# Attention, GLU and soft-MoE on one core: the value products of both blocks of a pair of heads in one group

## The chip, the core and the metric

The kernel runs on one NeuronCore of a Trainium2 chip. A core has five engines that run their own streams of instructions and meet at semaphores: TensorE (PE: matmuls and transposes), VectorE (DVE), ScalarE (ACT), GpSimd (POOL) and SyncE (SP), which here does nothing but issue DMAs. Matmuls write to PSUM, from where ACT and DVE copy results to SBUF. The metric is the device time of one execution in microseconds (us); a profiled execution, in which a hardware profiler records each instruction, gives the trace.

## What is computed

```python
attn = softmax(causal(q @ k.T / sqrt(D)) + decay_bias(s)) @ v    # B, H, S, D = 4, 8, 576, 64
x = attn, heads side by side                                      # 2304 tokens x 512
x = ((x @ w1) * (x @ w2)) @ w3 @ w_out                            # 512 -> 1024 -> 1024 -> 512
logits = x @ phi                                                  # 8 experts with 4 slots each
slots = softmax(logits over tokens).T @ x
y = relu(slot @ ew1[e]) @ ew2[e]                                  # for each expert's slots
out = softmax(logits over slots) @ y
```

The bias of a pair of positions is the difference of a running sum of max(s, 0), cut at zero. The weights of the middle part come as 64-bit floats.

## The kernel before, in words

**Items.** Attention goes through 40 items (ITEMS, L265). The 576 tokens of a head are five tiles: tile 0 has 64 tokens, tiles 1 to 4 have 128 each (QT, L32). Items 0 to 15 are the eight heads of batch 0 in two halves: tiles 0, 1, 2 of each head, then tiles 3 and 4. Items 16 to 39 are heads 8 to 31 with all five tiles. Heads 2m and 2m+1 make a pair, so there are twelve pairs of whole heads, items 16/17 to 38/39. The tokens lie in two blocks (BLK, L34): block 0 is tiles 0 to 2, 320 tokens; block 1 is tiles 3 and 4, 256 tokens.

**Steps of an item.** `att_scores` (L341) multiplies q and k: PE writes the sum of a product with `qa` and one with `qb` to `sc_ps`; DVE (L344) adds the mask and takes the row maximum nmax; ACT (L349) takes the exponential. `att_norm` divides on POOL (L362). `att_transpose` turns the result on PE (L377, `pt_ps`), copied by ACT to `pt` (L379), and the diagonal parts (L391, `ptd_ps`), copied to `ptd` (L393). `att_pv` (L395 on) multiplies by the values v.

**The value products.** For a pair n, n+1 and one block, `att_pv` takes an accumulator `x_ps` from the two PSUM buffers with the tag `acc` (PB, L78: four of tag `sg` for `sc_ps` and `gl`, two of `acc`, two of `tp`). Each product of the first head (e = 0) writes partitions 0 to 63, its twin of the second head (e = 1) partitions 64 to 127. Block 0 has ten products, block 1 twelve; each is two MATMUL records in the trace, as the operands are f32. `group` (L104) gives a list of products a high priority and chains them so that their order holds. The first of a list waits in addition for the copies of pt and ptd of both heads. Behind the products ACT copies the accumulator to `x[:, 0]` (L426, a CAST), and DVE writes the rest to `x[:, 1]` (L427). z_ps and ct_ps of the soft-MoE use the same two buffers of tag `acc`.

**What runs beside it.** While the items of one batch go on, the GLU of an earlier batch runs (`glu_half`, L430: twelve products `gl` to one buffer of `sg`, L439; ACT copies the first half to `a`, L445; DVE multiplies, L457, to gT, gU or gC), the soft-MoE's sums (`slot_...` functions: `gn_ps`, `lg`, `z_ps`, `ct_ps`), and the conversion of the weights: SP fetches words (L178, `raw_w`, `raw_wo`, `raw_w3t`), ACT (L186, L197) and DVE (L198, L201) convert them, SP stores some (L229).

**What sets the order.** `att_steps` writes a list of steps with a cost each; `weave` (L677) merges two lists in the ratio of their costs, and a scheduler turns this program into an order for PE, ACT, DVE and POOL, using priorities and its own picture of when operands are ready. SP alone keeps the order of the program. Its order in each item is: the values of a pair (L290, two buffers `v`, so that it waits for the value products of the pair two before), the decay rows for `qb` (L306), q and k (`raw`, L282), words (L178). When the last items are done, the loads of the tail begin with L828, whose place waits for the last value product.

Of the kernel before, what the change touches and what calls it, by code (L numbers as in the profile page):

```python
# [10 lines left out]
F32 = mybir.dt.float32  # L11
# [5 lines left out]
ALU = mybir.AluOpType  # L17
# [30 lines left out]
def attn_glu_softmoe_kernel(  # L48
# [31 lines left out]
    def psum(tag, name):  # L80
        return ps.tile([P, 512], F32, tag=tag, name=name, bufs=PB[tag])
# [310 lines left out]
                t["diag", j] = k  # L392
            t["turned", "d"] = nc.scalar.copy(out=ptd[:, : len(own)].rearrange("p j q -> p (j q)"), in_=dg[:, 64 : 64 * len(own) + 64])  # L393

    def att_pv(n, blk):  # L395

        b, c = divmod(ITEMS[n][0] // 2, H // 2)
        t0, nt, tiles = BLK[blk]
        acc = psum("acc", f"x_ps_{n}_{blk}")
        products = []  # L400

        def add(cols, weights, vs, start, stop):
            for e in range(2):
                t = hd[n + e]
                products.append((acc[64 * e : 64 * e + 64, cols], vs(t["v"], e), weights(t), start, stop))

        def diag(i, start, stop):
            d0 = sum(QT[i]) - 64 - t0
            add(slice(d0, d0 + 64), lambda t: t["ptd"][:, t["diag", i]], lambda v, e: v[:, 2 * i, e], start, stop)

        if tiles[0] == 0:
            diag(0, True, True)
        for j in range(tiles[-1]):

            own = [i for i in tiles if i > j]
            p0 = PT[own[0]][0] + PT[own[0]][1] * j
            add(
                slice(QT[own[0]][0] - t0, sum(QT[own[-1]]) - t0),
                lambda t: t["pt"][:, p0 : p0 + len(own)].rearrange("p i q -> p (i q)"),
                lambda v, e: v[:, 2 * j + 1, e], j == 0, False,  # L420
            )
        for i in tiles[-2:]:
            diag(i, False, i == tiles[-1])
        group(products, [hd[n + e]["turned", i] for e in range(2) for i in (tiles[-1], "d")])
        x = x_t[b, blk, c]
        nc.scalar.copy(out=x[:, 0], in_=acc[:, :nt])  # L426
        nc.vector.tensor_tensor(out=x[:, 1], in0=acc[:, :nt], in1=x[:, 0].bitcast(F32), op=ALU.subtract)  # L427


    gts = {}  # L430
# [207 lines left out]
    def att_steps(ap):  # L638

        groups = [[] for _ in range(B + 1)]  # L640
        N = len(ITEMS)
        for n in range(N + 1):
            tiles = ITEMS[n][1] if n < N else ()
            old = [i for i in ITEMS[n - 1][1] if i] if 0 < n <= N else []
            sc = [(0.2 + 0.3 * i, lambda i=i, n=n: att_scores(n, i, ap)) for i in tiles]
            tr = [(0.2 + 0.3 * i, lambda i=i, n=n: att_transpose(n - 1, i, ap)) for i in old]
            norm = [(0, lambda n=n: att_norm(n - 1))] if 0 < n <= N else []
            prep = [(0, lambda n=n: att_values(n + 1, ap))] if n + 1 < N else []
            d = FAR if n + FAR < NF32 else 1 if NF32 <= n + 1 < N else 0
            if d:  # L650
                prep += [(0, lambda m=n + d: att_prep(m, ap))]
            d = FAR + 1 if n + FAR + 1 < NF32 else 2 if NF32 <= n + 2 < N else 0
            if d:
                prep += [(0, lambda m=n + d: att_fetch(m, ap))]
            blks = [k for k in range(2) if BLK[k][2][0] in ITEMS[n - 1][1]]
            pv = [(1.4, lambda n=n, k=k: att_pv(n - 2, k)) for k in blks] if n > 0 and n % 2 == 0 else []
            groups[min(B, max(0, (n - 1) // H))] += [
                *sc[:1], *norm, *sc[1:2], *prep, *sc[2:3], *tr[:1], *sc[3:4], *tr[1:2], *sc[4:], *tr[2:], *pv
            ]
        return groups  # L660
# [457 lines left out]
```

## Time and profile before

| | |
|---|---|
| median of 3 runs | 562.74 us (562.33 to 567.34) |
| profiled execution, its own time | 565.44 us |
| its span in the trace | 563.6 us |
| mean granted clock of TensorE | 0.981 of full speed |
| instructions | 11844, of them 4288 MATMUL records |
| PE busy | 520.0 us, 92% of the span |
| weight loads (PEld), which overlap PE | 433.9 us |
| DVE, ACT, POOL busy | 316.2, 310.0, 196.7 us |
| bytes moved | 118.03 MB, 209 GB/s over the span |

The page gives one line per view; in the timeline a row is a run of like instructions, with its start, its length, engine, line, operation, tiles and count, and in brackets the idle time of the engine just before it and what ended it. PE's matmuls are pipelined, so the length of a row reaches into the next; the distance of two starts is what a piece of work costs. In the list of waits stands the idle time of an engine in front of a line, summed, with how often and the longest.

### The profile page before, as it was taken

To read this page: it belongs to the slowest core of one execution; us is meant where nothing else is said; L and a number is where in the kernel's file an instruction comes from. 1 tells how busy PE (TensorE), PEld (TensorE's weight loads), DVE (VectorE), ACT (ScalarE), POOL (GpSimd) and SP (SyncE) were. 2 spreads that over 40 slices of the span, in tenths; PEclk is the share of its full clock that TensorE was granted. 3 is DMA by queue.
4 is the path that set the end of the run, shared out by engine and by line. 5 is a ranking of instruction groups with operands and counts; after the bars stand their busy time and mean duration, and the time that the engine had idled before them with its cause. 6 is when DMAs were issued, how large, how long until landed. Compare 5 with 4: busy or idle time off the path is not lost. (4 is left out here: it accounts for less than half of the span.)

```text
span 563.6 us, 11844 instructions
## 1 busy us (share of the span) xinstructions
PE 520.0 (92%) x4288; PEld 433.9 (77%) x4288; DVE 316.2 (56%) x966; ACT 310.0 (55%) x845; POOL 196.7 (35%) x247
## 2 busy tenths in 40 slices
PE   3789899998979999899899999999999999999993
PEld 2566688787768897889889889889988999853452
DVE  7568696889964385736574657446631311243333
ACT  4576586788865675646566567357833321321222
POOL 5475464438745374253354444333210000000000
PEclk9997899999979999999999999999999999999998
DMA  5765966868654173345646563555330999689977
GB/s 157 237 179 178 261 203 215 287 219 261 191 201 119 39 220 109 130 135 179 206 136 213 168 197 104 166 167 172 113 113 1 391 413 381 233 300 421 421 296 244
DMA packets 38809, 118.03 MB, mean 209 GB/s; under 512 B 4224, under 2 KB 10560, under 8 KB 35296
## 3 DMA queue, kind: packets, MB, share of 16 engines
q1 hardware_dynamic: 36832, 113.74, 58.8%
q10 hardware_dynamic: 1920, 3.54, 2.5%
q8 instruction: 34, 0.56, 0.4%
q14 instruction: 23, 0.19, 0.1%
HBM read 102.11 MB, written 11.60 MB: 202 GB/s over the span
## 5 line engine op out<-in xcount | busy, mean ns | idle before, releaser
L439 PE MATMUL gl<-x,w12t 128*128 128x320 f32 (+1 forms) x1536 | 238.3, 304 | 1.3 <-DVE nmax L344 0.7
L439 PEld LDWEIGHTS gl<-x,w12t 128*128 128x128 f32 x1536 | 212.2, 191 | 10.0 <-issue 4.3
L362 POOL TENSOR_SCALAR sc<-sc,rinv 128x64 f32<-128x64 f32 (+4 forms) x160 | 92.4, 594 | 53.9 <-DVE rinv L359 39.2
L349 ACT ACTIVATE sc<-sc,nmax 128x64 f32<-128x64 f32 (+4 forms) x160 | 89.5, 560 | 32.2 <-DVE nmax L344 31.6
L317 POOL TENSOR_TENSOR qa<-raw,qa 64x576 fp32r<-64x576 f32 x24 | 36.5, 1522 | 144.1 <-DVE qa L311 138.3
L344 DVE CUSTOM_DVE_ANT_0 sc<-sc_ps,mask 128x64 f32<-128x64 f32 (+4 forms) x160 | 64.8, 424 | 32.1 <-PE sc_ps L341 29.0
L379 ACT COPY pt<-pt_ps 128x128 f32<-128x128 f32 (+3 forms) x128 | 52.2, 423 | 27.1 <-PE pt_ps L377 16.3
L377 PE MATMUL pt_ps<-ident,sc 128*128 128x128 f32 x320 | 56.8, 288 | 4.9 <-ACT pt L379 2.3
L341 PE MATMUL sc_ps<-qa 128*128 128x64 f32 (+1 forms) x144 | 46.6, 336 | 6.0 <-DVE nmax L344 2.5
L377 PEld LDWEIGHTS pt_ps<-ident,sc 128*128 128x128 f32 x320 | 38.8, 145 | 17.3 <-issue 10.0
L341 PE MATMUL sc_ps<-qb 68*128 68x64 f32 (+1 forms) x144 | 44.2, 310 | 4.2 <-issue 4.2
L110 PE MATMUL x_ps<-pt,v 128*64 128x256 f32 (+1 forms) x384 | 47.5, 353 | 0.0
L445 ACT COPY a<-gl 128x256 f32<-128x256 f32 (+1 forms) x64 | 25.3, 398 | 38.5 <-PE gl L439 34.8
L341 PE MATMUL sc_ps<-raw 68*128 68x288 f32 (+4 forms) x96 | 35.5, 514 | 11.1 <-DMA raw<-rows 9.6
L990 POOL MEMSET ht<- 128x1024 f32 x2 | 1.9, 954 | 107.3 <-DVE ew L894 98.4
L186 ACT ACTIVATE w_w<-raw_w 128x512 f32<-128x512 f32 x32 | 21.6, 676 | 31.6 <-DMA raw_w<-in_w 31.6
L314 POOL TENSOR_TENSOR qb<-raw,qa 64x576 fp32r<-64x576 f32 x24 | 38.2, 1590 | 2.2 <-PE gl L439 0.5
L110 PEld LDWEIGHTS x_ps<-pt,v 128*64 128x64 f32 x384 | 32.0, 138 | 6.7 <-issue 1.0
L341 PEld LDWEIGHTS sc_ps<-qa 128*128 128x128 f32 x144 | 27.7, 192 | 9.1 <-DVE nmax L344 3.5
L427 DVE TENSOR_TENSOR x<-x_ps,x 128x320 fp32r<-128x320 f32 (+1 forms) x32 | 14.0, 455 | 36.2 <-ACT x L426 36.1
L341 PEld LDWEIGHTS sc_ps<-raw 68*128 68x128 f32 x96 | 21.2, 259 | 16.3 <-issue 12.1
L341 PEld LDWEIGHTS sc_ps<-qb 68*128 68x128 f32 x144 | 28.0, 194 | 4.6 <-issue 4.4
(180 smaller groups left out, 785.4 us busy)
## 6 DMA issues: line engine op xcount, KB each, us to landing
ew<-in_ew SPq DMA_DIRECT2D x27, 1024.0 KB
raw_w<-in_w SPq DMA_DIRECT2D x32, 512.0 KB
raw<-in_qk SPq DMA_DIRECT2D x24, 576.0 KB
v<-in_v SPq DMA_DIRECT2D x16, 576.0 KB
raw_w3t<-in_w3t SPq DMA_DIRECT2D x16, 512.0 KB
raw_wot<-in_wot SPq DMA_DIRECT2D x8, 512.0 KB
raw_wo<-in_wo SPq DMA_DIRECT2D x8, 512.0 KB
w_d<-w_w SPq DMA_DIRECT2D x8, 512.0 KB
```

The costliest lines, as they stand in the source:

```text
L110: mm = nc.tensor.matmul(out_, lhs, rhs, start=start, stop=stop)
L186: nc.scalar.activation(out=w, in_=hi.bitcast(F32), func=AF.Copy, scale=F64_SCALE)
L314: nc.gpsimd.tensor_tensor(out=qb[0:64, 1, :q1], in0=rk[0:64, :q1], in1=qa[0:64, 1, :q1].bitcast(F32), op=ALU.subtract)
L317: nc.gpsimd.tensor_tensor(out=qa[64:, 0, q0:q1], in0=rq[64:, q0:q1], in1=qa[64:, 0, q0:q1].bitcast(F32), op=ALU.subtract)
L341: nc.tensor.matmul(pp[:r, : z - a], x[:, 0, q0 : q0 + r], x[:, 1, a:z], start=x is mul[0], stop=x is mul[-1])
L344: nc.vector.tensor_tensor_reduce(out=sc[:r, a:z], in0=pp[:r, : z - a], in1=hd["mask"][:r, m0 : m0 + z - a], scale=-0.125, scalar=3.0e38 if ...
L349: nc.scalar.activation(out=sc[:r, :W], in_=sc[:r, :W], func=AF.Exp, bias=nmax[:r, i : i + 1], scale=-1.0, accum_out=rsum[:r, i, 0:1],)
L362: nc.gpsimd.tensor_scalar(out=sc, in0=sc, scalar1=rinv[:, i : i + 1], scalar2=1.0, op0=ALU.mult, op1=ALU.mult)
L377: nc.tensor.transpose(tp[:, j * P : (j + 1) * P], sc[:, j * P : (j + 1) * P], ident)
L379: t["turned", i] = nc.scalar.copy(out=pt[:, p0 : p0 + step * (i - 1) + 1 : step], in_=tp[:, : i * P].rearrange("p (j q) -> p j q", q=P))
L439: nc.tensor.matmul(acc[:, :nt], w12_t[fc][:, wi, n, kc], x_t[b, blk, kc][:, xi], start=k == 0, stop=k == 3 * KC - 1)
L445: nc.scalar.copy(out=a_sb[:, :nt], in_=acc[:, :nt])
```

## The change

`att_pv` takes a list of blocks in place of one. For the pairs of items 0 to 15, which have one block each, the program is as it was. For the twelve pairs of items 16 to 39 one call makes both blocks: it takes both `acc` buffers, puts the 22 products in one list, block 0 first, and hands them to one `group`; behind it stand the copy and the subtraction of block 0, then those of block 1. The first product waits for the turned copies of the last tile of both heads and of ptd. In `att_steps` one step of cost 2.8 stands where two of 1.4 stood. The lines behind `att_pv` move down by five: L439 of before is L444 of after, L426 is L431.

```diff
-    def att_pv(n, blk):
+    def att_pv(n, blks):
         b, c = divmod(ITEMS[n][0] // 2, H // 2)
-        t0, nt, tiles = BLK[blk]
-        acc = psum("acc", f"x_ps_{n}_{blk}")
-        products = []
+        products, accs = [], {}
+        for blk in blks:
+            t0, nt, tiles = BLK[blk]
+            acc = accs[blk] = psum("acc", f"x_ps_{n}_{blk}")
...
-        group(products, [hd[n + e]["turned", i] for e in range(2) for i in (tiles[-1], "d")])
-        x = x_t[b, blk, c]
-        nc.scalar.copy(out=x[:, 0], in_=acc[:, :nt])
-        nc.vector.tensor_tensor(out=x[:, 1], in0=acc[:, :nt], in1=x[:, 0].bitcast(F32), op=ALU.subtract)
+        last = BLK[blks[-1]][2][-1]
+        group(products, [hd[n + e]["turned", i] for e in range(2) for i in (last, "d")])
+        for blk in blks:
+            nt, acc, x = BLK[blk][1], accs[blk], x_t[b, blk, c]
+            nc.scalar.copy(out=x[:, 0], in_=acc[:, :nt])
+            nc.vector.tensor_tensor(out=x[:, 1], in0=acc[:, :nt], in1=x[:, 0].bitcast(F32), op=ALU.subtract)
...
-            pv = [(1.4, lambda n=n, k=k: att_pv(n - 2, k)) for k in blks] if n > 0 and n % 2 == 0 else []
+            pv = [(1.4 * len(blks), lambda n=n, k=blks: att_pv(n - 2, k))] if n > 0 and n % 2 == 0 else []
```

The order of POOL is the same in both kernels, and that of SP too but for names of buffers. ACT has 703 rows and DVE 944 in both, in another order. PE has 1803 rows before and 1814 after.

The first place is items 30/31 on PE (x_ps_0 is block 0, x_ps_1 block 1; numbers behind the names tell buffers apart; ptd_3874 and pt_3873 are of head 0 of the pair, ptd_4030 and pt_4029 of head 1; lg_1 is a sum of the soft-MoE). Before:

```order
L110 MATMUL x_ps_0_4128<-ptd_3874,v_3627 64x64
L110 MATMUL x_ps_1_4156<-pt_3873,v_3627 64x256
L110 MATMUL lg_1_4286<-gT_1_0_3515,v_sb 32x256
L110 MATMUL lg_1_4286<-gT_1_1_3563,v_sb 32x256
L110 MATMUL lg_1_4286<-gT_1_2_3682,v_sb 32x256
L110 MATMUL lg_1_4286<-gT_1_3_3784,v_sb 32x256
L110 MATMUL lg_1_4286<-gU_1_4_3940,v_sb 32x256 x2
L110 MATMUL lg_1_4286<-gU_1_6_4113,v_sb 32x256 x2
L110 MATMUL x_ps_1_4156<-pt_4029,v_3627 64x256
```

After:

```order
L110 MATMUL lg_1_4286<-gT_1_0_3515,v_sb 32x256
L110 MATMUL lg_1_4286<-gT_1_1_3563,v_sb 32x256
L110 MATMUL lg_1_4286<-gT_1_2_3682,v_sb 32x256
L110 MATMUL lg_1_4286<-gT_1_3_3799,v_sb 32x256
L110 MATMUL lg_1_4286<-gU_1_4_3940,v_sb 32x256 x2
L110 MATMUL lg_1_4286<-gU_1_6_4113,v_sb 32x256 x2
L110 MATMUL x_ps_0_4128<-ptd_3874,v_3627 64x64
L377 MATMUL pt_ps_1_4237<-ident,sc_3983 128x128
L110 MATMUL x_ps_0_4128<-ptd_4030,v_3627 64x64
L110 MATMUL x_ps_0_4128<-pt_3873,v_3627 64x256
L110 MATMUL x_ps_0_4128<-pt_4029,v_3627 64x256
```

The eight lg products, which stood between the first two products and the others, now stand ahead of the pair. The first product of head 0 stands alone, with one transpose behind it, and then the other 21 stand in a row.

The second place is items 24/25 on PE (gl_0_4_1 and gl_0_5_0 are two halves of a GLU of block 0, with 12 products each; sc_ps_0_0 and sc_ps_1_0 are the scores of tiles 0 and 1 of the item after next). Before:

```order
L439 MATMUL gl_0_4_1_3202<-x_0_1_1312,w12t_662 128x320 x3
L110 MATMUL x_ps_0_3041<-ptd_2774,v_2576 64x64
L110 MATMUL x_ps_1_3059<-pt_2773,v_2576 64x256
L110 MATMUL x_ps_0_3041<-ptd_2939,v_2576 64x64
L110 MATMUL x_ps_0_3041<-pt_2773,v_2576 64x256
L110 MATMUL x_ps_0_3041<-pt_2938,v_2576 64x256
L110 MATMUL x_ps_0_3041<-pt_2773,v_2576 64x128
L110 MATMUL x_ps_0_3041<-pt_2938,v_2576 64x128
L110 MATMUL x_ps_1_3059<-pt_2938,v_2576 64x256
```

After:

```order
L444 MATMUL gl_0_4_1_3202<-x_0_3_1960,w12t_662 128x320 x3
L341 MATMUL sc_ps_0_0_3232<-qa_3124 128x64
L341 MATMUL sc_ps_0_0_3232<-qb_3123 128x64
L444 MATMUL gl_0_5_0_3237<-x_0_0_1090,w12t_759 128x320 x3
L444 MATMUL gl_0_5_0_3237<-x_0_1_1312,w12t_759 128x320 x3
L444 MATMUL gl_0_5_0_3237<-x_0_2_1623,w12t_759 128x320 x3
L444 MATMUL gl_0_5_0_3237<-x_0_3_1960,w12t_759 128x320 x2
L110 MATMUL x_ps_0_3041<-ptd_2774,v_2576 64x64
L444 MATMUL gl_0_5_0_3237<-x_0_3_1960,w12t_759 128x320
L341 MATMUL sc_ps_1_0_3260<-qa_3124 128x192
L110 MATMUL x_ps_0_3041<-ptd_2939,v_2576 64x64
L110 MATMUL x_ps_0_3041<-pt_2773,v_2576 64x256
```

The products stood behind six of the twelve gl_0_4_1; now they stand behind all of them, behind the scores of tile 0, behind the twelve gl_0_5_0 and one product of the scores of tile 1. On ACT, at the same place (w_wo and raw_wo are words of the weights; pt and ptd are copies of transposes), before:

```order
L426 CAST x_0_0_2267<-x_ps_0_3041 128x320
L426 CAST x_1_0_2268<-x_ps_1_3059 128x256
L379 COPY pt_3144<-pt_ps_1_3146 128x128
L379 COPY pt_3144<-pt_ps_2_3169 128x2x128
L349 ACTIVATE sc_3231,rsum_94<-sc_3231,nmax_3230 128x64
L445 COPY a_0_5_3250<-gl_0_5_0_3237 128x320
L379 COPY pt_3144<-pt_ps_3_3197 128x3x128
L379 COPY pt_3144<-pt_ps_4_3217 128x4x128
L349 ACTIVATE sc_3231,rsum_94<-sc_3231,nmax_3230 128x192
L349 ACTIVATE sc_3231,rsum_94<-sc_3231,nmax_3230 128x320
L186 ACTIVATE w_wo_3341<-raw_wo_0_3337 128x512
```

After:

```order
L349 ACTIVATE sc_3231,rsum_94<-sc_3231,nmax_3230 128x64
L450 COPY a_0_5_3250<-gl_0_5_0_3237 128x320
L431 CAST x_0_0_2267<-x_ps_0_3041 128x320
L431 CAST x_1_0_2268<-x_ps_1_3042 128x256
L379 COPY pt_3144<-pt_ps_1_3146 128x128
L379 COPY pt_3144<-pt_ps_2_3169 128x2x128
L349 ACTIVATE sc_3231,rsum_94<-sc_3231,nmax_3230 128x192
L349 ACTIVATE sc_3231,rsum_94<-sc_3231,nmax_3230 128x320
L379 COPY pt_3144<-pt_ps_3_3197 128x3x128
L349 ACTIVATE sc_3231,rsum_94<-sc_3231,nmax_3230 128x448
L379 COPY pt_3144<-pt_ps_4_3217 128x4x128
L186 ACTIVATE w_wo_3341<-raw_wo_0_3337 128x512
```

The two copies out of x_ps stand behind an exponential and a copy of gl that stood behind them; and one exponential, 448 wide, now stands ahead of the word w_wo where it stood behind.

## Rows read from the trace of the kernel before

**Rows 1.** The page's busy times: engine, us (share of the span), instructions.
```profile
span 563.6 us, 11844 instructions
PE 520.0 (92%) x4288; PEld 433.9 (77%) x4288; DVE 316.2 (56%) x966; ACT 310.0 (55%) x845; POOL 196.7 (35%) x247
```

**Rows 2.** Windows: length, busy us of PE, PEld, DVE, ACT, POOL, granted clock, DMA share, GB/s.
```profile
150.00:200.00 50.00, 45.56 (x431) 38.89 (x429) 27.97 (x98) 31.61 (x95) 23.79 (x29) 0.93 0.41 130
...
435.00:470.00 35.00, 35.00 (x275) 33.17 (x271) 7.88 (x22) 9.55 (x25) 0.00 (x0) 1.00 0.97 382
```

**Rows 3.** Waits of PE between 144 and 437 us: us in total, times, longest.
```profile
PE sc_ps L341 <- DVE nmax L344: 2.5, 2, 1.4
PE sc_ps L341 <- DVE gC L457: 2.4, 2, 2.1
```

**Rows 4.** Windows with the tile x_ps alone: PE's busy us first, its records in brackets.
```profile
144.00:151.00 7.00, 3.93 (x44) 2.74 (x44) 0.00 (x0) 0.00 (x0) 1.00 0.51 169
...
192.00:197.00 5.00, 2.97 (x44) 2.44 (x44) 0.49 (x1) 0.42 (x1) 1.00 0.04 5
...
378.00:383.00 5.00, 3.33 (x44) 2.90 (x44) 0.00 (x0) 0.00 (x0) 1.00 0.53 175
...
sum 72.00, PE 39.94 PEld 33.15 DVE 6.43 ACT 6.03; mean PE 3.33 PEld 2.76 DVE 0.54 ACT 0.50
```

**Rows 5.** Timeline of PE at items 30/31.
```profile
324.95 0.33 PE L110 MATMUL x_ps<-ptd,v 128*64 128x64 f32 x2
325.12 0.60 PE L110 MATMUL x_ps<-pt,v 128*64 128x256 f32 x2
326.50 0.64 PE L110 MATMUL lg<-gT,v_sb 128*32 128x256 f32 x8 [0.78 <-DVE nmax L344]
```

**Rows 6.** Timeline of PE at items 36/37.
```profile
414.12 0.33 PE L110 MATMUL x_ps<-ptd,v 128*64 128x64 f32 x2
414.38 0.50 PE L439 MATMUL gl<-x,w12t 128*128 128x256 f32 x2
414.81 0.27 PE L110 MATMUL x_ps<-ptd,v 128*64 128x64 f32 x1
...
415.95 1.91 PE L110 MATMUL z_ps<-gn,dT 128*32 128x512 f32 x12
...
419.81 1.74 PE L110 MATMUL x_ps<-pt,v 128*64 128x256 f32 x16
...
421.71 1.46 PE L439 MATMUL gl<-x,w12t 128*128 128x256 f32 x10
```

**Rows 7.** Timeline of all engines, 150 to 163 us: SP's DMA for qb, PE's wait.
```profile
153.28 0.28 SPq L306 DMA_DIRECT2D qb<-rows_d  x1
...
161.21 0.39 PE L341 MATMUL sc_ps<-qb 68*128 68x64 f32 x1 [4.21 <-issue]
```

**Rows 8.** Waits of SP's queue: us in total, times, longest.
```profile
SPq L828 <- PE x_ps L110: 20.9, 1, 20.9
```

**Rows 9.** Timeline of SP's queue: DMA issues at items 24 to 27.
```profile
250.94 0.89 SPq L178 DMA_DIRECT2D raw_wo<-in_wo  x2
...
275.58 0.33 SPq L229 DMA_DIRECT2D wo_d<-w_wo  x1
275.96 0.42 SPq L290 DMA_DIRECT2D v<-in_v  x1
```

**Rows 10.** Timeline of ACT, 255 to 275 us.
```profile
258.11 0.66 ACT L186 ACTIVATE w_wo<-raw_wo 128x512 f32<-128x512 f32 x1 [2.04 <-DMA raw_wo<-in_wo]
...
271.01 0.70 ACT L186 ACTIVATE w_wo<-raw_wo 128x512 f32<-128x512 f32 x1 [3.15 <-DMA raw_wo<-in_wo]
...
274.12 0.74 ACT L426 CAST x<-x_ps 128x320 fp32r<-128x320 f32 x2
```

**Rows 11.** Timeline of PE, 250 to 272 us.
```profile
250.41 2.00 PE L439 MATMUL gl<-x,w12t 128*128 128x320 f32 x12
252.34 1.06 PE L110 MATMUL z_ps<-gn,dT 128*32 128x512 f32 x8
...
271.73 0.42 PE L341 MATMUL sc_ps<-qa 128*128 128x320 f32 x1
```

More of the change, by code (lines that the diff above doesn't have):

```diff
@@ L393, in att_transpose @@
             t["turned", "d"] = nc.scalar.copy(out=ptd[:, : len(own)].rearrange("p j q -> p (j q)"), in_=dg[:, 64 : 64 * len(own) + 64])
-    def att_pv(n, blk):
+    def att_pv(n, blks):
         b, c = divmod(ITEMS[n][0] // 2, H // 2)
-        t0, nt, tiles = BLK[blk]
-        acc = psum("acc", f"x_ps_{n}_{blk}")
-        products = []
[L402 to L423, printed above, removed]
-        group(products, [hd[n + e]["turned", i] for e in range(2) for i in (tiles[-1], "d")])
-        x = x_t[b, blk, c]
-        nc.scalar.copy(out=x[:, 0], in_=acc[:, :nt])
-        nc.vector.tensor_tensor(out=x[:, 1], in0=acc[:, :nt], in1=x[:, 0].bitcast(F32), op=ALU.subtract)
@@ new lines, in att_pv, with add, diag @@
+        products, accs = [], {}
+        for blk in blks:
+            t0, nt, tiles = BLK[blk]
+            acc = accs[blk] = psum("acc", f"x_ps_{n}_{blk}")
+            def add(cols, weights, vs, start, stop):
+                for e in range(2):
+                    t = hd[n + e]
+                    products.append((acc[64 * e : 64 * e + 64, cols], vs(t["v"], e), weights(t), start, stop))
+            def diag(i, start, stop):
+                d0 = sum(QT[i]) - 64 - t0
+                add(
+                    slice(d0, d0 + 64), lambda t: t["ptd"][:, t["diag", i]], lambda v, e: v[:, 2 * i, e], start, stop
+                )
+            if tiles[0] == 0:
+                diag(0, True, True)
+            for j in range(tiles[-1]):
+                own = [i for i in tiles if i > j]
+                p0 = PT[own[0]][0] + PT[own[0]][1] * j
+                add(
+                    slice(QT[own[0]][0] - t0, sum(QT[own[-1]]) - t0),
+                    lambda t: t["pt"][:, p0 : p0 + len(own)].rearrange("p i q -> p (i q)"),
+                    lambda v, e: v[:, 2 * j + 1, e], j == 0, False,
+                )
+            for i in tiles[-2:]:
+                diag(i, False, i == tiles[-1])
```

## The prediction

> **What bounds the kernel now.** I read the page's busy times first: TensorE (PE) has work in 520.0 of the 563.6 us of the span [rows 1]. The table by stages shows where the rest bites: 45.56 of 50 us busy from 150 to 200 us, with a granted clock of 0.93, and from 435 us on, where attention is over, 35.00 of 35 us beside DMA at 0.97 [rows 2]. So during attention the span is the sum of what PE does, one instruction behind the other, and what it waits. The list of SP's waits says that the tail's loads hang on attention's end: the first of them (L828) waited 20.9 us, for the last value product [rows 8]. Time won or lost on PE before 435 us is therefore passed on to the tail whole; the tail itself is untouched by the diff.
>
> The list of PE's waits between 144 and 437 us, the stretch of the twelve pairs, holds some 13 us; the two causes shown in [rows 3] are the second and third largest. They end with VectorE (DVE), but DVE stood behind ScalarE (ACT), and ACT behind the words of weights that a DMA brings: ACT waits 2.04 us at 258.11 and 3.15 us at 271.01 for raw_wo [rows 10]. The largest single wait is 4.21 us at 161.21 [rows 7]: PE wants rows of a qb whose DMA left SP only at 153.28.
>
> **The change part by part.** No product, copy or subtraction is added or taken away; 22 products of a pair that stood in two groups now stand in one, and both accumulators are taken ahead of it.
>
> *The products.* The table by windows for the tile x_ps gives PE's busy time in each of twelve pairs: 39.94 us in all, 3.33 us a pair, from 2.97 (at 192 us) to 3.93 (at 144 us) [rows 4]. The order of before is cut by other work in eight places, and where the two groups are interleaved the products of the two heads do not stand side by side. Of the order after: in eleven of the twelve pairs the first product of head 0, 64 columns wide, stands alone ahead of one or two other rows, then the other 21 run unbroken. Its price from starts: 0.17 us for the lone product (324.95 to 325.12) [rows 5]; the rest of block 0, 414.81 to 415.95, 1.14; block 1 alone, 419.81 to 421.71, 1.90 [rows 6]. That is 3.2 us with a switch behind each of the three pieces, of which one falls away, so I take 3.1. Twelve pairs at 3.1 are 37.2, against 39.94: **-2.7 us**. The bounds: all pairs as the shortest of before, 12 x 2.97 = 35.6, -4.3; all pairs as the pair at 378 us, where block 0 is already closed ahead of block 1, 12 x 3.33 = 40.0, no gain.
>
> How much a break costs: a lone product starts at 414.12 and the gl product behind it at 414.38, 0.26 us [rows 6], against the 0.17 us where an x_ps product follows; so a change of kind is dearer by 0.09. Breaks rise from eight to eleven, three more, two changes of kind each: 0.5 us, which is within the 3.1 above, since its pieces hold their breaks. The Trainium skill, "TensorEngine Tiling (Array Packing)", in the section on key properties, says that a change of the tiling mode, not of the tile alone, drains TensorE; the x_ps products, 64 columns wide, stand between products of 128. By that rule the change works against itself at the lone product; if the 0.5 us came on top, the sum below would be 563.0. The 0.09 us agrees with a short drain and no more.
>
> *The first pair's gain.* The pair at 144 us costs 3.93, so 0.8 us of the 2.7 come from it. But behind it stands the wait of 4.21 us that ends at 161.21 with qb's rows, and that DMA's place in SP's queue is unmoved: PE only waits longer. **+0.8 us**, bounds 0 and 0.8.
>
> *Products that come later.* SP's queue keeps its order. The value fetch (L290) needs a buffer that the pair two before must have read, and behind it in SP's queue stand the decay rows (L306), q and k of the next item (L282) and two words (L178). In the order of PE the group of three pairs now stands behind more work: items 24/25 behind 18 gl products and three score products, 26/27 behind 24 gl and eight score products, 28/29 behind 14 gl. Twelve gl of 320 columns take 1.93 us from 250.41 to 252.34, 0.16 each [rows 11], so 0.13 for 256 columns as an estimate; score products I put at 0.1 for the narrow ones and 0.2 for the others, the start at 161.21 to the next being 0.20. That makes 3.2, 4.7 and 1.8 us later. What of it reaches the words: all of the first, since words leave at 250.94 right behind that pair. Of the second little: the value fetch at 275.96 went behind a store of weights at 275.58 [rows 9], and the pair's products were over at 271.73, where a score product starts [rows 11], so 271.7 + 4.7 = 276.4 makes it 0.4 later. All of the third. Sum 5.4 us of later transfers. At the first of them the new order of ACT has an exponential (448 wide) and two copies of pt ahead of the words, some 1.6 us of work that PE's next steps need, so 3.8 us of more waiting remain on ACT. What PE loses of it: behind ACT's wait of 3.15 PE waited at most 1.4, the longest for nmax, which is 0.44 of it [rows 3, 10]. 3.8 x 0.44 = **+1.7 us**. Bounds: 0, if PE's work ahead covers it, and 5.4, if it is passed on whole.
>
> *Evacuations.* Per pair, ACT's two copies (L426) and DVE's two subtractions (L427) now come after all 22 products. Block 0's copy may start some 1.9 us later than it could; nothing reads x of a pair until its batch's GLU begins, so I put this at nothing. Where that cover is gone, the second accumulator costs the wait of rival C. The merged step counts 2.8 in the weaving, as two steps of 1.4 did; what this moves is in the orders already.
>
> **Sum**: -2.7 + 0.8 + 1.7 = -0.2 us on the profiled execution, whose own time is 565.44 (span 563.6, 1.8 around it): 565.2. That execution is 2.7 us above the median of 562.74, so against the median **562.5 us**: a real gain on PE which the transfers take back. The likeliest case by itself spans 559 to 566: -4.3 + 0.8 at best, 0.0 + 0.8 + 1.7 at worst, with a little around both.
>
> **The rivals.** One per cent, 5.6 us, is about what a measurement of this kernel can tell from no change.
>
> A: the new order also takes PE's waits away. The waits of 2.1 (for gC), 1.4 (for nmax) and 0.78 us (at 326.50) [rows 3, 5] all come from work placed behind an ACT that waits for a word; in the new order at items 24/25 an exponential and two copies now stand ahead of the words. If all three go, and none of the 1.7: -2.7 + 0.8 - 4.3 = -6.2, **556.5 us**. For it: the order puts more gl products ahead where PE waited. Against it: the first of them stands ahead of items 24/25, where no group of products has moved far.
>
> B, on the other side: the later fetch at 24/25 starves ACT, and PE's clock falls. ACT's wait of 2.04 grows by 3.2 to 5.2 us; passed on whole to PE, it is longer than the 4.21 after which the granted clock fell: the stretch 150 to 200 has 0.93 [rows 2], 7% of 50 us, 3.5 us. With the first pair's loss, -2.7 + 0.8 + 5.4 + 3.5 = +7.0, **569.7 us**. It decides from the point where PE's own wait there reaches some 4 us. Against it: PE has gl products of its own to do meanwhile.
>
> C: two accumulators taken at once starve the next user. z_ps and ct_ps share the two buffers. The copy out of x_ps at 274.12 came 2.5 us after the last product [rows 10], as ACT stood at the words; where z_ps or ct_ps is next, PE now waits for that. At four places: -2.7 + 0.8 + 4 x 2.5 = +8.1, **570.8 us**. In the trace of before PE waits nowhere for an x_ps buffer, and the order after puts gl products or transposes behind x_ps at most pairs. The Trainium skill, "Perfetto Trace Analysis", section on matmuls, speaks for this rival: independent groups should go round PSUM's banks so that the copy-out of one overlaps the next group's products. Here this merged group takes both; no row of before shows such a wait.
>
> D: the tighter group brings nothing (3.33 a pair) and the fetches still come later: 0.8 falls away with the gain, +1.7, **564.4 us**.
>
> **How the numbers follow.** The forecast 0.58, A 0.19, B 0.12, C 0.06, D 0.05. The forecast and D lie within 1% (0.63), and about 0.02 of A, which ends at the edge; so faster 0.17, within 1% 0.65, slower 0.18 (B and C). The range from 555.5 to 568.5 takes in the forecast, D, most of A and the lower edge of B, some 0.8.
>
> **What would show it.** Right: the x_ps products sum to about 37 us over twelve windows, with starts of a pair 2.9 to 3.2 apart; the wait near 161 us ends at the same time with about 0.8 more idle; the words behind items 24/25 leave SP near 254 us, ACT's wait for them near 260 is over 3 us, and PE's waits in 144 to 437 sum to some 15 us. Wrong: PE's waits under 10 us (A), a second fall of the granted clock between 250 and 310 us (B), waits of z_ps or ct_ps for a copy of x (C), or an x_ps sum near 40 us (D). The forecast is off, too, if the tail's DMA-bound loads do not follow the end of attention.

## The result, and the profile after

| | before | after |
|---|---|---|
| median | 565.23 us (20 runs, 560.59 to 571.20) | 569.42 us (20 runs, 564.78 to 575.43) |
| ratio | | 1.0071 (95%: 1.0043 to 1.0098) |
| profiled execution, its own time | 565.44 us | 567.02 us |
| its span | 563.6 us | 565.2 us |
| mean granted clock | 0.981 | 0.988 |

The changed kernel is slower by 0.7%, some 4 us: within the 1% that was called no change, but beyond the interval, and on the other side of the 0.2 us that were forecast as a gain. The time of 569.42 us lies 0.9 us above the range. A part of that is the level: over 20 runs the kernel before measured 565.23, where the three runs that the forecast was set against had a median of 562.74.

The busy time of PE after, from the page (the line that answers to [rows 1]):

```profile
span 565.2 us, 11850 instructions
PE 521.4 (92%) x4288; PEld 438.9 (78%) x4288; DVE 309.2 (55%) x966; ACT 311.6 (55%) x845; POOL 197.1 (35%) x247
```

PE is busy 1.4 us longer, with the same number of products. The products of values, from the table by windows for the tile x_ps (PE's busy us in each window first; this answers to [rows 4]):

```profile
191.00:196.00 5.00, 3.29 (x44) 3.01 (x44) 0.49 (x1) 0.43 (x1) 1.00 0.13 31
...
sum 66.00, PE 39.45 PEld 36.14 DVE 6.29 ACT 6.27; mean PE 3.29 PEld 3.01 DVE 0.52 ACT 0.52
```

All twelve pairs now read 3.29, and the sum is 39.45 against 39.94 before: a gain of 0.5 us where the forecast had 2.7. The waits of PE from 144 to 437 us (total, times, longest; this answers to [rows 3]) are others than before:

```profile
PE pt_ps L377 <- ACT gn L617: 3.2, 3, 2.4
PE w3ts_ps L257 <- ACT w3tp L249: 2.7, 1, 2.7
PE l L499 <- ACT ls L479: 1.7, 1, 1.7
PE sc_ps L341 <- DVE nmax L344: 1.5, 1, 1.5
```

The wait of 4.21 us near 161 us has turned into one of 2.7 for another operand that comes just before; the two near 239 and 276 us, 2.1 and 1.4, are gone but for 0.7 us; and two new ones stand near 288 us. The score product of [rows 7], ahead of which the 4.21 us stood, starts at the same time as before:

```profile
161.21 0.40 PE L341 MATMUL sc_ps<-qb 68*128 68x64 f32 x1
```

Where the idle time lies shows in windows: length, then PE's busy us; the difference of the two is idle time. After, first trace:

```profile
200.00:225.00 25.00, 23.88 (x210) 20.59 (x209) 12.70 (x42) 15.02 (x41) 11.18 (x14) 1.00 0.42 134
225.00:275.00 50.00, 49.27 (x392) 46.63 (x392) 28.03 (x89) 28.39 (x83) 19.43 (x23) 1.00 0.46 152
275.00:300.00 25.00, 20.68 (x166) 18.75 (x162) 14.09 (x42) 16.79 (x48) 8.34 (x13) 0.93 0.51 170
...
sum 296.00, PE 282.00 PEld 257.13 DVE 160.91 ACT 180.08 POOL 115.26; mean PE 47.00 PEld 42.85 DVE 26.82 ACT 30.01 POOL 19.21
```

The same windows of the kernel before, first trace:

```profile
200.00:225.00 25.00, 24.89 (x217) 21.82 (x216) 16.41 (x48) 16.47 (x47) 14.27 (x20) 1.00 0.47 154
225.00:275.00 50.00, 47.91 (x392) 44.90 (x390) 27.66 (x83) 29.47 (x83) 17.04 (x21) 1.00 0.47 152
275.00:300.00 25.00, 22.41 (x187) 19.94 (x187) 17.33 (x55) 16.34 (x48) 12.12 (x15) 1.00 0.54 170
...
sum 296.00, PE 282.91 PEld 253.86 DVE 166.18 ACT 181.88 POOL 115.20; mean PE 47.15 PEld 42.31 DVE 27.70 ACT 30.31 POOL 19.20
```

From 275 to 300 us PE is idle 4.3 us after (25.00 - 20.68) against 2.6 before, and the granted clock is 0.93; from 200 to 225 us 1.1 against 0.1; from 225 to 275 us 0.7 against 2.1. What happens at 288 us is in the timelines of SP (two words of weights leave at 280.74 us), ACT and PE (start, length, in brackets the idle time before and what ended it):

```profile
278.56 0.33 SPq L229 DMA_DIRECT2D wo_d<-w_wo  x1
...
280.74 0.93 SPq L178 DMA_DIRECT2D raw_w<-in_w  x2
```

```profile
288.05 0.66 ACT L186 ACTIVATE w_w<-raw_w 128x512 f32<-128x512 f32 x1 [4.46 <-DMA raw_w<-in_w]
...
289.15 0.57 ACT L617 COPY gn<-gn_ps 128x512 f32<-128x512 f32 x1
...
291.49 0.43 ACT L479 COPY ls<-lg 128x320 f32<-128x320 f32 x1
```

```profile
285.68 0.33 PE L377 MATMUL pt_ps<-ident,sc 128*128 128x128 f32 x1
285.77 1.67 PE L444 MATMUL gl<-x,w12t 128*128 128x256 f32 x12
289.87 0.41 PE L377 MATMUL pt_ps<-ident,sc 128*128 128x128 f32 x2 [2.43 <-ACT gn L617]
291.97 0.93 PE L499 MATMUL l<-ls,sel 128*128 128x320 f32 x2 [1.69 <-ACT ls L479]
292.37 3.08 PE L444 MATMUL gl<-x,w12t 128*128 128x256 f32 x12
```

The same place in the kernel before, on SP, ACT and PE:

```profile
277.83 0.88 SPq L178 DMA_DIRECT2D raw_w<-in_w  x2
```

```profile
285.62 0.67 ACT L186 ACTIVATE w_w<-raw_w 128x512 f32<-128x512 f32 x1 [1.78 <-DMA raw_w<-in_w]
```

```profile
288.00 0.33 PE L377 MATMUL pt_ps<-ident,sc 128*128 128x128 f32 x1
288.93 0.41 PE L377 MATMUL pt_ps<-ident,sc 128*128 128x128 f32 x2 [0.60 <-ACT gn L612]
289.09 1.67 PE L439 MATMUL gl<-x,w12t 128*128 128x256 f32 x12
290.94 0.81 PE L494 MATMUL l<-ls,sel 128*128 128x320 f32 x2 [0.18 <-ACT ls L474]
```

After, ACT stands 4.46 us for a word. Behind it stands the copy gn, which frees a buffer of the transposes, and PE waits 2.43 us for it; behind both words stands the copy ls, and PE waits 1.69 for that. Two things differ from before: the words leave 2.9 us later, while PE is 2.3 us further on (285.68 against 288.00), and the twelve gl products that covered the wait for ls (289.09) now stand ahead of the transposes (285.77). Then twelve gl products take 3.08 us at half the clock. The window of that stretch shows it (the last number but two is the granted clock): 3.4 us at 0.50, a loss of 1.7:

```profile
292.50:295.90 3.40, 3.40 (x18) 3.25 (x17) 1.66 (x6) 0.84 (x3) 2.55 (x5) 0.50 0.59 185
```

The row behind attention's last product starts 1.65 us later than before (437.49 against 435.84 us), and the span is 1.6 us longer: what follows takes 127.8 us before and 127.7 after, so the delay was passed on whole, as forecast.

### The profile page after: what moved, and what is told of

Same layout as the page of the kernel before. It is cut to its first block, busy times and chain, and to the rows that moved or that the text cites. A ratio compares the mean times of both kernels' runs of the same rounds, so it can differ in the third digit from the quotient of the medians.

```text
span 565.2 us, 11850 instructions
## 1 busy us (share of the span) xinstructions
PE 521.4 (92%) x4288; PEld 438.9 (78%) x4288; DVE 309.2 (55%) x966; ACT 311.6 (55%) x845; POOL 197.1 (35%) x247
## 4 chain that ended last, share of the span: by engine, by line
PE 59%; DMA 21%; ACT 7%; DVE 7%; issue 2%; SPq 1%; POOL 1%; ACTq 0%; DVEq 0%; POOLq 0%
PE gl L444 23%; DMA raw_w<-in_w 10%; PE x_ps L110 8%; PE sc_ps L341 6%; DMA raw_w3t<-in_w3t 5%; PE pt_ps L377 4%; PE o_ps L1024 3%; PE h_ps L986 3%; PE gn_ps L614 2%; DMA raw_wo<-in_wo 2%; PE ptd_ps L391 2%; DMA raw_wot<-in_wot 2%; PE z_ps L110 2%; ACT sc L349 2%; DVE sc L344 1%
## 5 line engine op out<-in xcount | busy, mean ns | idle before, releaser
L444 PE MATMUL gl<-x,w12t 128*128 128x320 f32 (+1 forms) x1536 | 239.9, 305 | 2.3 <-DVE nmax L344 1.7
L444 PEld LDWEIGHTS gl<-x,w12t 128*128 128x128 f32 x1536 | 212.7, 190 | 13.8 <-issue 7.1
L110 PEld LDWEIGHTS x_ps<-pt,v 128*64 128x64 f32 x384 | 37.0, 140 | 3.1 <-issue 1.0
L341 PEld LDWEIGHTS sc_ps<-raw 68*128 68x128 f32 x96 | 21.4, 263 | 15.4 <-issue 12.6
L617 ACT COPY gn<-gn_ps 128x512 f32<-128x512 f32 x40 | 22.7, 585 | 16.6 <-PE gn_ps L614 16.5
```

The costliest lines, as they stand in the source:

```text
L110: mm = nc.tensor.matmul(out_, lhs, rhs, start=start, stop=stop)
L341: nc.tensor.matmul(pp[:r, : z - a], x[:, 0, q0 : q0 + r], x[:, 1, a:z], start=x is mul[0], stop=x is mul[-1])
L444: nc.tensor.matmul(acc[:, :nt], w12_t[fc][:, wi, n, kc], x_t[b, blk, kc][:, xi], start=k == 0, stop=k == 3 * KC - 1)
L617: st["turned", blk, k, h] = nc.scalar.copy(out=gn[:r, 4 * h : 4 * h + 4].rearrange("p c f -> p (c f)"), in_=tp[:r])
```

## The experiments

A letter stands for each theory in the expectations. W: the late words near 288 us make the time. R: the new order of items 16 to 22 makes it. P: the merged group is dearer on PE. C: chance, by which a wait is or isn't followed by a fall of the clock. Later G: the group has a cost of its own; O: any new order that the planner makes around the products costs or gains by chance. Each ratio sets 6 to 12 runs against 17 to 35 runs of the kernel before on the same chip.

| kernel | ratio | 95% interval |
|---|---|---|
| changed kernel again | 1.0098 | 1.0068 to 1.0128 |
| merged for items 16 to 23 alone | 1.0083 | 1.0053 to 1.0114 |
| merged for items 24 to 29 alone | 1.0052 | 1.0020 to 1.0085 |
| merged for items 30 to 39 alone | 1.0041 | 1.0017 to 1.0066 |
| before again | 1.0011 | 0.9981 to 1.0041 |
| two groups, values one item later from item 16 | 1.0101 | 1.0068 to 1.0134 |
| one group, the same | 1.0003 | 0.9969 to 1.0037 |
| two groups, values one item later from item 24 | 1.0041 | 1.0012 to 1.0070 |
| one group, the same | 1.0041 | 1.0011 to 1.0072 |
| two groups, second head first | 0.9959 | 0.9926 to 0.9993 |
| one group, second head first | 0.9990 | 0.9954 to 1.0026 |
| one group, second head first, values later from 24 | 1.0027 | 1.0000 to 1.0054 |
| two groups, cost of a step 0.7 | 1.0134 | 1.0089 to 1.0179 |
| one group, the same | 1.0050 | 1.0018 to 1.0083 |
| two groups, cost of a step 2.1 | 1.0193 | 1.0152 to 1.0233 |
| one group, the same | 1.0131 | 1.0078 to 1.0183 |

**The changed kernel again, and its parts.** The changed kernel unaltered, and three kernels in which only some pairs are merged:

```diff
-            pv = [(1.4 * len(blks), lambda n=n, k=blks: att_pv(n - 2, k))] if n > 0 and n % 2 == 0 else []
+            cut = [blks] if n - 2 < 24 else [[k] for k in blks]        # or 24 <= n - 2 < 30, or n - 2 >= 30
+            pv = [(1.4 * len(s), lambda n=n, k=s: att_pv(n - 2, k)) for s in cut] if n > 0 and n % 2 == 0 else []
```

> The changed kernel once more, nothing altered, for a second trace and more times. Theory W (words: the products of items 24/25 and 26/27 end later, so the value fetch and the words behind it leave SP later, ACT stands longer for raw_w near 288 us, PE waits some 4 us there, and TensorE's clock falls behind it): 1.006 to 1.008 of the kernel before, and this trace again shows waits of some 4 us on PE between 286 and 293 us with the granted clock at half for some us right behind. Theory R (the order around items 16 to 22, and nothing at 288, makes the time): the same ratio, but the waits near 288 us are not there every time. Theory P (the merged group itself is dearer on PE): the x_ps starts of a pair are 3.15 us apart as in the first trace, which is 0.6 us less than before over all pairs, so P would need a ratio under 1.000.

> Only the four pairs of items 16 to 23 stand in one group; the eight pairs from item 24 on have two groups as before. In PE's order items 24/25 stand at the same late place as in the changed kernel (behind twelve gl of block 0, second half of the fifth, and the score of the next item's tile 0), items 26/27 twelve rows earlier than in the changed kernel. Theory W: the lateness comes with the order of items 16 to 23, so words leave late at 24/25 and most of the loss is here, 1.003 to 1.008. Theory R: all of it, 1.006 to 1.008. Theory P: a third of it, 1.002.

> Only the three pairs of items 24 to 29 stand in one group. In PE's order items 24/25 stand where they stood before, items 26/27 a few rows earlier than before. Theory W: words leave as early as before, 0.998 to 1.002, and no wait over 2.5 us near 288 us. Theory R: 1.000, as items 16 to 22 are in the old order. Theory P: a quarter of it, 1.002.

> Only the five pairs of items 30 to 39 stand in one group. Theory W: 0.998 to 1.002, since nothing ahead of item 30 has moved. Theory R: 1.000. Theory P: five twelfths of the loss, 1.003. If the loss is somewhere behind item 30, this one has it: 1.005 or more.

The changed kernel repeated its loss, and its trace the waits of 1.5 and 1.7 us near 288 us with the clock at 0.93 from 275 to 300 us. Its windows:

```profile
275.00:300.00 25.00, 21.79 (x177) 20.00 (x174) 15.17 (x45) 16.52 (x48) 8.06 (x13) 0.93 0.51 170
...
sum 296.00, PE 280.71 PEld 255.70 DVE 160.20 ACT 178.99 POOL 115.81; mean PE 46.78 PEld 42.62 DVE 26.70 ACT 29.83 POOL 19.30
```

The idle time is 296.00 - 280.71 = 15.3 us from 144 to 440 us (14.0 in the first trace). But the parts do not add up: 0.83, 0.52 and 0.41% make 1.8%, and the whole costs 0.7 to 1.0%, a difference somewhat beyond the intervals. R wanted 1.000 for the second and the third part, which lies outside both intervals; W wanted at most 1.002 there, which lies at their lower edges. P wanted a third, a quarter and five twelfths (1.002, 1.002 and 1.003) and misses the first part; it also wanted the whole under 1.000. The part of items 30 to 39 shows why one trace is not enough. Up to item 30 its order is that of the kernel before on PE, ACT and DVE alike. Its windows from 236 to 248 us, then those of the kernel before in two traces:

```profile
236.00:248.00 12.00, 9.72 (x50) 9.42 (x50) 7.38 (x27) 5.15 (x19) 4.67 (x7) 0.72 0.28 94
```

```profile
236.00:248.00 12.00, 9.94 (x87) 9.31 (x87) 7.33 (x29) 5.77 (x19) 7.42 (x12) 1.00 0.34 107
```

```profile
236.00:248.00 12.00, 11.43 (x87) 10.87 (x89) 5.22 (x24) 4.98 (x15) 7.36 (x12) 0.86 0.34 107
```

The same order, a wait of 2.28, 2.06 and 1.56 us in the same place, and a granted clock of 0.72, 1.00 and 0.86 (the last of the waits began ahead of the window): the first trace of the kernel before was one in which the clock did not fall there.

**The kernel before again, and the value fetch out of the words' way.** The kernel before unaltered; and in both kernels SP's fetch of the values moved one item later, behind the words, from item 16 or from item 24 on:

```diff
-            prep = [(0, lambda n=n: att_values(n + 1, ap))] if n + 1 < N else []
+            prep = [(0, lambda m=n + (n < 16): att_values(m, ap))] if n < N else []      # or n < 24
```

> The kernel before, with one thing moved: from item 16 on the value fetch of a pair is issued one item later, behind the words of that item, so that SP no longer stands for the products of the pair two before with the rows, q and k and words behind it. Theory W (the words behind the value fetch make the time): words leave SP earlier, the waits of ACT for raw_wo and raw_w fall from some 2 to 3 us each to under 1, PE's waits between 200 and 300 us fall from 5 to under 3 us: 0.990 to 0.997. Theory R (the order of items 16 to 22): 0.998 to 1.002. Theory C (which waits are followed by a fall of the clock decides, and chance has a large part): anything from 0.995 to 1.005, with the same number of falls as before.

> The changed kernel with the same one thing moved. Theory W: with the words out of the way of the products, the merged group costs nothing any more; within 0.3% of the kernel before with the late value fetch, and 0.99 to 0.997 of the kernel before; no wait over 2 us on PE near 288 us and no fall of the clock there. Theory R: still 0.6 to 0.8% above the kernel before with the late value fetch. Theory C: above it by what its extra falls cost, 1.7 to 3.4 us each.

> The kernel before once more, unaltered: a second trace, and a measure of what two samples of one kernel differ by. Every theory: 0.997 to 1.003. Theory C (chance in the clock falls has a large part): this trace shows a fall at another place than the first, for instance near 239 us, where two traces with the same order of instructions had one and the first trace of this kernel had none. Theory W: PE's waits between 270 and 300 us stay under 3 us and no fall follows there.

> The kernel before with the value fetch one item later from item 24 on alone, so that everything ahead of item 24 is as before (the variant from item 16 on lost some 4 us ahead of the first of the twelve pairs, which has nothing to do with the words of items 24 on). Theory W: words of items 24 to 29 no longer wait for products; 0.994 to 1.000. Theory R: 1.000.

> The changed kernel with the same late value fetch from item 24 on. Items 16 to 23 stand as in the changed kernel. Theory W: the waits near 288 us and the fall behind them go, and with them 4 to 6 us of the changed kernel: 0.996 to 1.002 of the kernel before. Theory R: the loss is made by the order of items 16 to 23 and stays: 1.006 to 1.010.

The wait near 288 us went, as W had expected. Windows of the changed kernel with the value fetch later from item 24 on:

```profile
200.00:225.00 25.00, 23.11 (x201) 19.69 (x199) 12.25 (x39) 13.75 (x36) 11.18 (x14) 1.00 0.52 167
...
275.00:300.00 25.00, 24.46 (x210) 22.54 (x208) 15.87 (x51) 17.11 (x50) 11.29 (x14) 1.00 0.51 164
300.00:360.00 60.00, 56.26 (x453) 51.40 (x450) 34.74 (x116) 35.13 (x100) 22.32 (x29) 0.97 0.49 153
...
sum 296.00, PE 282.19 PEld 256.57 DVE 159.51 ACT 179.28 POOL 112.17; mean PE 47.03 PEld 42.76 DVE 26.59 ACT 29.88 POOL 18.69
```

From 275 to 300 us PE is idle 0.5 us (4.3 and 3.2 without the move) at full clock. Its words left at 279.51 us, only 1.2 us earlier than without the move, and the order of PE there is another too, so it is not shown that the fetch alone did this. But from 200 to 225 us it is idle 1.9 and from 300 to 360 us 3.7, and the total of idle time, 13.8 us, is as before the move (14.0 and 15.3). The kernel gained 0.3 to 0.6%, not the whole loss; and the same move, which frees words from the products, made the kernel with two groups slower by 0.4% (1.0% from item 16 on), where W wanted a gain. Of the 1.0% most is lost ahead of the twelve pairs, and not at the words: in that trace the first pair starts at 149.49 us, where it starts at 144.55 and 143.98 in the two traces of the kernel before. With the fetch moved, one group against two is 1.0041 to 1.0041, and 1.0003 to 1.0101: no loss by the group, or a gain. W names a real wait, but that wait alone is not the cause of the time. The kernel before against itself was 1.0011, with an interval 0.3% to either side; its second trace has 9.2 us of idle time where the first has 13.1:

```profile
275.00:300.00 25.00, 23.03 (x174) 20.69 (x176) 16.85 (x53) 16.71 (x49) 11.29 (x14) 0.93 0.54 170
...
sum 296.00, PE 286.76 PEld 258.20 DVE 166.27 ACT 181.40 POOL 115.15; mean PE 47.79 PEld 43.03 DVE 27.71 ACT 30.23 POOL 19.19
```

and its clock, too, fell between 275 and 300 us, behind 2.0 us of idle time. So the fall there is not what sets the changed kernel apart. Cut at the start of the first of the twelve pairs and at the row behind attention's last product, the traces of the kernel before, then of the changed one, give:

```profile
144.55:435.84 291.29, 278.20 (x2405) 249.36 (x2404) 164.27 (x523) 177.80 (x501) 114.65 (x145) 0.99 0.45 146
```

```profile
143.98:434.66 290.68, 281.44 (x2405) 252.98 (x2404) 164.22 (x523) 177.59 (x501) 115.17 (x145) 0.98 0.45 146
```

```profile
144.21:437.49 293.28, 279.28 (x2405) 254.51 (x2404) 159.96 (x524) 178.15 (x499) 115.05 (x145) 0.98 0.44 145
```

```profile
143.53:438.50 294.97, 279.54 (x2404) 254.39 (x2404) 160.24 (x524) 178.47 (x499) 116.28 (x145) 0.98 0.44 144
```

The length falls into three terms: idle time, what half the clock costs, counted as half of the time for which the trace grants it, and the rest.

| us | before | before again | changed | changed again |
|---|---|---|---|---|
| length of the stretch | 291.3 | 290.7 | 293.3 | 295.0 |
| PE idle | 13.1 | 9.2 | 14.0 | 15.4 |
| lost at half the clock | 3.4 | 6.8 | 5.1 | 5.1 |
| PE's work at full clock | 274.8 | 274.6 | 274.2 | 274.4 |

In the mean of two traces each the changed kernel is 3.1 us longer here: 3.6 us more idle time, the same loss of clock, 0.4 us less work. What follows takes 127.7 or 127.8 us in all four.

**The second head first.** In the order of the changed kernel the first product of a pair stands alone, as it needs nothing of the second head, whose copies come last. With the second head first it has to wait for these, and nothing gets in between:

```diff
-                for e in range(2):
+                for e in (1, 0):
```

> The changed kernel with the two heads of each product in the other order: the second head first. The first product of the list then waits for the last copies, so that nothing stands between it and the other 21; in PE's order all twelve pairs are unbroken rows of 22. Theory P (the form of the products): a pair falls from 3.15 to about 2.75 us from start to start, twelve pairs save 4 to 5 us, and the kernel comes to 0.998 to 1.002 of the kernel before. Theory W: the saving on PE is there, but the words stay late and the wait near 288 us stays; half of the saving at most reaches the end: 1.003 to 1.007.

> The kernel before, two groups per pair, with the second head first in each product. In PE's order eleven of the twelve pairs are unbroken rows of 22, one is cut between the blocks. Theory P: pairs fall to 2.7 to 2.9 us, 4 to 5 us less over twelve pairs, 0.991 to 0.996. Theory W: its products stand about where those of the kernel with one group and this order stand, so words leave as late as there: 1.000 to 1.007, and like the kernel with one group and this order within 0.2%.

> One group per pair, second head first, and the late value fetch from item 24 on. Theory W: both gains add, 0.4% or more under the kernel with that order alone: 0.990 to 0.995 of the kernel before, as fast as two groups with the second head first. Theory R: as without the late fetch, 0.997 to 1.001.

The timeline of PE at items 24/25 of the changed kernel, and of the one with the second head first:

```profile
247.70 0.33 PE L110 MATMUL x_ps<-ptd,v 128*64 128x64 f32 x2
247.96 0.42 PE L444 MATMUL gl<-x,w12t 128*128 128x320 f32 x1
...
248.39 0.27 PE L110 MATMUL x_ps<-ptd,v 128*64 128x64 f32 x1
248.40 0.43 PE L110 MATMUL x_ps<-pt,v 128*64 128x256 f32 x1
...
251.28 0.44 PE L377 MATMUL pt_ps<-ident,sc 128*128 128x128 f32 x2
```

```profile
245.81 0.34 PE L110 MATMUL x_ps<-ptd,v 128*64 128x64 f32 x4
...
248.70 0.55 PE L377 MATMUL pt_ps<-ident,sc 128*128 128x128 f32 x3
```

0.26 and 2.89 make 3.15 us with the lone product; unbroken it is 2.89. Twelve pairs at 0.25 less are 3 us. PE's work at full clock in the stretch of the twelve pairs, worked out as above, is 270.5 us with one group (274.2 and 274.4 without the edit) and 271.0 with two (274.8 and 274.6), and the kernel with one group came from 1.0071 and 1.0098 to 0.9990, some 4 us: P's mechanism holds for the lone product, though not for one group against two. With two groups the same edit made the fastest kernel of all, 0.9959, 562.2 us. The one group has in this setting the waits near 288 us again (1.90 and 1.69 us). Its words left at 277.95 us, by the clock as early as in the kernel before (277.83), but PE was further on: the first of these transposes starts at 283.15 us, where it starts at 288.00 in the kernel before. So the words are late against PE's own place, as in the changed kernel, and its order of PE is that of the changed kernel too, with the twelve gl products ahead of the transposes. With the late value fetch added the words left at 273.69 us, and 0.6 us of the waits was left under that same order of PE, though another of ACT. This speaks for the lateness of the words; what the place of the gl products adds, no run shows apart. The kernel did not become faster by it (1.0027, intervals overlap): both gains do not add.

**Controls: another order, the same work.** The weaving's cost of a step of value products was changed from 1.4 to 0.7 and to 2.1, with two groups and with one:

```diff
-            pv = [(1.4, lambda n=n, k=k: att_pv(n - 2, k)) for k in blks] if n > 0 and n % 2 == 0 else []
+            pv = [(0.7, lambda n=n, k=k: att_pv(n - 2, k)) for k in blks] if n > 0 and n % 2 == 0 else []
```

> A control: the kernel before, with the cost that the weaving gives to a step of value products halved (0.7 for 1.4). The work is the same; the planner makes another order. Theory O (any new order around the products loses or wins by chance, the kernel before having a good one, and the group itself costs nothing): 1.002 to 1.010, that is slower than the kernel before although no group is merged. Theory G (the merged group has a cost of its own, some 3 us): 0.997 to 1.003.

> The changed kernel, one group per pair, with the same halved cost of a step (0.7 per block). Theory O: anywhere between 0.998 and 1.010 of the kernel before, and above or below the two-group kernel with that cost as it falls. Theory G: 0.6% above the two-group kernel with that cost.

> A second control: two groups, the cost of a step 2.1 for 1.4. Theory O: 1.002 to 1.010. Theory G: 0.997 to 1.003.

> One group per pair, the cost of a step 2.1 per block. Theory O: 0.998 to 1.010, above or below the two-group kernel with that cost as it falls. Theory G: 0.6% above the two-group kernel with that cost.

The controls with two groups are 1.3 and 1.9% slower than the kernel before, though no product, copy or transfer is other than before; with one group they are 0.8 and 0.6% faster than with two. The windows of the control with 2.1:

```profile
360.00:440.00 80.00, 76.95 (x649) 69.30 (x648) 37.85 (x117) 42.39 (x117) 21.58 (x31) 0.98 0.40 129
sum 296.00, PE 280.97 PEld 252.11 DVE 171.78 ACT 177.34 POOL 118.99; mean PE 46.83 PEld 42.02 DVE 28.63 ACT 29.56 POOL 19.83
```

15.0 us idle, in other places (3.1 from 360 to 440 us, where the kernel before has 1.5). In the stretch of the twelve pairs the two controls move all three terms: 16.8 and 15.0 us idle, 10.2 and 5.1 lost at half the clock, 272.1 and 277.3 of work (0.7, then 2.1; 9.2 to 13.1, 3.4 to 6.8 and 274.6 to 274.8 in the kernel before). They also lose time ahead of it, where the change does nothing: their first pair starts at 147.8 and 146.4 us (144.0 and 144.6). G wanted these controls at 1.000 and the kernel with one group 0.6% above its control: it falls. One group against two, over the six settings: +0.7 to +1.0% (the change itself), +0.3, 0.0, -1.0, -0.8, -0.6%. The mean is -0.2%, and both signs occur; as the six scatter by 0.7%, a cost or gain of half a per cent would not be seen. So the merged group has no cost of its own that these runs show. What is left is that the loss of 0.7% is that of a new order against one that happens to fit; this is reached by elimination, and which of the moved pieces makes it is not shown.

## Why the prediction was wrong

**What bounds the kernel: right.** Time lost on PE ahead of 437 us reached the end whole: 1.65 us there, 1.6 us in the span.

**The term of the products: the step that failed.** It set 12 x 3.1 us, worked out from starts of rows, against 39.94, a sum of busy times in which the tail of each row counts as well. In starts, the pair at 246 us took 2.95 us before and takes 3.15 after; in busy time, where a pair reads 2.97 to 3.93 before [rows 4], all twelve are 39.94 against 39.45. In starts alone, idle time left out, the twelve take 38.7 us before and 37.9 after. Like set against like, the gain is 0.5 us in busy time or 0.8 in starts, not 2.7. The pieces were right: 3.15 measured for the 3.1 forecast, with the lone product in it. With 0.5 in the sum it would have read -0.5 + 0.8 + 1.7 = +2.0 us, a loss as measured; the first trace has +1.6. That this fits so well is in part luck: that execution of the changed kernel lies 2.4 us under its median, and the medians are 4.2 us apart. What the sum leaves of these 4.2 us stays open; by the two traces of each kernel it is mostly idle time. The lone product was counted as a switch of 0.09 us and the breaks as 0.5 us in all; its price is 0.25 us a pair, 3 us in all, as its twin of the other head then starts beside the next, wider product of the first head (248.39 and 248.40 us), and the two heads stay one product out of step. The Trainium skill, "TensorEngine Tiling (Array Packing)", key properties, speaks of a drain at a change of the tiling mode; whether one is part of the 0.25 us, no run here shows.

**The first pair's gain: about right.** The wait near 160 us ended at nearly the same time: the score product of [rows 7], which started at 161.21 us, starts at 161.21 in the first trace after, too. Ahead of it PE now waits 2.69 us for w3tp and then does other work.

**Products that come later: right in kind, wrong in place and reason.** Words behind items 24/25 left at 252.66 us instead of 250.94 [rows 9], 1.7 us later and not 3.2. The second transfer was put at 0.4 us later, with the store of weights at 275.58 [rows 9] taken as fixed. But the store waits for the words fetched before it to be converted, and these came later; it left at 278.56, and the words behind it at 280.74 instead of 277.83, 2.9 us later. ACT's waits for words grew to 2.25, 3.82 and 4.46 us where they were 2.04, 3.15 [rows 10] and 1.78. PE's idle time from the first pair to attention's end grew by 0.9 us in the first traces (14.0 for 13.1) and by 3.6 in the mean of two, where the forecast had 0.8 + 1.7 = 2.5. The place where it came, near 288 us, was not the one forecast: there the words were late, and the twelve gl products that had covered a wait stood ahead of it.

**The rivals.** A: two of its waits did go (2.1 and 1.4), and others came. B: the wait on ACT and the fall of the clock behind it came, near 288 us instead of 258, behind waits of 2.43 and 1.69 us instead of one of some 4, and cost 1.7 us of clock instead of 3.5; as the kernel before has such falls in its other execution, they do not carry the difference. C: no z_ps or ct_ps product of PE waited for a copy of x in the trace; one w3t_ps product, which uses the same buffers, waited 0.5 us for the subtraction. In the trace of before, too, one wot_ps product waited so, for 0.7 us and ahead of the twelve pairs, where the prediction says that none does. D: its term of the products (no gain) was nearer than the forecast's.

**What was missing.** There was no rival with the price that matters: that the planner's new order alone, with no part of the change named, moves the time by up to 1.9%. Its size could not be read from the rows of one trace, and idle time of the kernel before was taken from one execution as if it were fixed. The range also went by a median of three runs, 2.5 us under that of twenty.

## What to carry to other kernels

Set a difference of starts against a difference of starts; a busy time of pipelined matmuls is another measure, and a term that mixes them shows a gain that isn't there. Where a planner makes the order anew, an edit is to be judged over a few orders, with controls that change the order and not the work, before its own effect is believed: here one group against two went from +1.0 to -1.0% with the setting. What takes work away from the engine that bounds (second head first: 0.25 us a pair) showed in PE's work in both kernels that got it; the rearrangements moved the time by more than that, by up to 1.9%, but one way or the other with the setting.

## What the runs showed of the hardware

The same wait of some 2 us in the same order of instructions was followed by a fall of the granted clock in two traces (0.72 and 0.86 from 236 to 248 us) and by none in a third (1.00): a fall that one trace shows, or lacks, is no property of the kernel. And the products of two heads, which write the two halves of the partitions, run side by side, where they stand side by side in the order: a product of 64 columns that stands alone ahead of other work, with its twin behind that work, made a pair cost 3.15 instead of 2.89 us.
